# First element of a cached-attention decoder: key tiles scored and reloaded in halves, two more tiles scored earlier, 64 equal columns in the down sums

## The chip, the core and the metric

The kernel runs on one core of one Trainium2 chip, in one launch. The metric is the device time of an execution in microseconds; the times given are medians over runs. Five engines work side by side in a core: TensorE (PE in the profile, its weight loads PEld), VectorE (DVE), ScalarE (ACT), GpSimd (POOL) and SyncE (SP), which in this kernel issues nearly all transfers from HBM. The PE runs at a granted clock that the profile shows in two values, 1.0 and 0.5.

## The reference

Four batch elements, one token each, pass twice through an attention layer (A) and a gated feed-forward layer (B), with the same weights and the same caches both times:

```python
x = A_x                                                    # [4, 1, 512]
x = x + A(layernorm(x));  x = x + B(layernorm(x))
x = x + A(layernorm(x));  x = x + B(layernorm(x))

def A(x):   # 32 query heads on 8 key/value heads, 4096 cached keys, head size 128
    q = (x @ wq).reshape(B, 1, 32, 128).transpose(0, 2, 1, 3)
    k, v = repeat(k_cache, 4, axis=1), repeat(v_cache, 4, axis=1)
    p = softmax(q @ k.T * 128 ** -0.5)
    return (p @ v).reshape(B, 1, 4096) @ wo

def B(x):   # 512 -> 1792 -> 512
    return (gelu(x @ w_gate) * (x @ w_up)) @ w_down
```

All of it is bfloat16. The key cache and the value cache hold 4 x 8 x 4096 x 128 numbers each, 33.5 MB apiece.

## The kernel before, in words

**Units.** A key or value head of one element is two tiles (t = 0 and 1, `last` is 1) of 128 partitions x 16 chunks (`CH`) x 128, 512 KB each: a row of 4096 bytes in each partition. Eight heads make two groups of four (`GH`); for one element and one layer the groups are handled one after the other, called `gx` and `gy`. All tiles of an element's second pass over attention that still lie in SBUF from the first pass are used again, in reversed group order; the rest is loaded again.

**Scores.** `scores_of` (L586) multiplies a key tile by the query block `qb`: four matmuls a tile (`BE`, the loop over `be`), each with 512 moving columns and 32 output rows. Head s writes rows 32s to 32s+31 of the one PSUM tile `sc`, so the matmuls of up to four heads run side by side in the four 32-column strips of the PE; two heads alone use two strips. `qb` is filled by `q_sums_of` (L349, PE) and `q_spread` (L357, DVE) from the rounded query rows `q_bf` of `q_round` (L333, DVE).

**The order of the work** is written out by hand. Each engine runs its instructions in the order of the program, and SP issues the transfers in the order in which they stand. A transfer into a tile waits on SP until the last reader of that place has finished, and all that is behind it on SP waits too. Eight semaphores go round among SP's transfers: one is issued when the transfer eight before it has landed.

**First element, second pass.** `attend_first` (L959) does the first attention of element 0 and then issues all weights (`load_rest`, L158), the down weights `wd_sb` last, and three key tiles of element 1 (`Early`, L1039). `dense_first` (L1314) is the feed-forward layer: gate (L1339), up (L1343), and `down` (L485), 56 matmuls of `wd_sb` with one hidden column repeated to `WIDE` = 32 equal moving columns. `OutProj` (L376) has such repeated columns too, there `WEIGHT` = 64 of them. `busy` (L479) runs matmuls whose result nobody reads. Then `Early.queries` (L1057) makes the query rows of `gx` in two halves of the heads (heads 2 and 3 of the group first), and `Early.scores` (L1089) scores the key tiles of element 0 that were kept in SBUF:

1. `first([(2, 0), (3, 0)])`, and the loads of two key tiles of element 1 into their places;
2. `self.rest()`: query sums and spread for heads 0 and 1;
3. `q = qy()`: the query rows of the other group, `q_rows` (L321): 16 matmuls of 512 columns in all four strips, a DVE transpose of 512 columns, `q_round`;
4. `first([(2, last), (3, last), (0, 0), (1, 0)])`, two more loads, and copies of parked key tiles back from PSUM and spare SBUF (`Parked.back`, L561) by DVE, GpSimd and ScalarE;
5. `first([(0, last), (1, last)])`, a fifth load, more copies; then softmax.

In `attend` (L1135) follow the scores of `gy` (L1170), each with four further loads (L1171), and the value tiles through a ring of eight places (`VRing.pump`, L692).

Of the kernel before, what the change touches and what calls it, by code (L numbers as in the profile page):

```python
# [15 lines left out]
P = 128  # L16
# [3 lines left out]
QS = P // QD  # L20
WIDE = 32
WEIGHT = 64
# [4 lines left out]
CH = 16  # L27
# [9 lines left out]
def kernel(  # L37
# [13 lines left out]
    nc = tc.nc  # L51
# [7 lines left out]
    KD = D // P  # L59
# [8 lines left out]
    W = 4 * QD  # L68
# [20 lines left out]
    dq = nc.sync  # L89
# [5 lines left out]
    wd_sb = wts.tile([P, KF, D], BF16, name="wd_sb")  # L95
# [22 lines left out]
    qb = const.tile([P, W + NK * 2 * W], BF16, name="qb")  # L118
    cs_f = const.tile([P, 2, KF], FP32, name="cs_f")

    place = {(s, t): (KW[s], t) for s in range(GH) for t in range(NT)}
    place.update({(GH + s, t): (KP[t][s // 2], s % 2) for s in range(GH) for t in range(NT)})

    def k_tile(i, t):
        pair, n = place[i, t]
        return pair[:, n]

    def acc(shape, name, t=None):
        if t is None:
            t = ps_ac.tile([P, 512], FP32, name=name, tag="acc")  # L130
        n = 1
        for s in shape:
            n *= s
        if len(shape) == 1:
            return t[:, :n]
        return t[:, :n].rearrange("p (a b) -> p a b", b=shape[1])

    def wide(v, width=WIDE):
        n = v.shape[-1]
        return v.unsqueeze(1).broadcast_to([P, width // n, n])  # L140

    def whole(b, kvh):
        return b == 0 and kvh < GH
# [5 lines left out]
    def cache_tile(cache, b, kvh, t):  # L149
        if whole(b, kvh):  # L150
            return cache[b, kvh].rearrange("(p t c) d -> t p c d", t=NT, p=P)[t]
        return cache[b, kvh].rearrange("(t p c) d -> t p c d", t=NT, p=P)[t]
# [121 lines left out]
    def mac(dst, lhsT, rhs, first, last):  # L274
        nc.tensor.matmul(dst, lhsT=lhsT, rhs=rhs, start=first, stop=last, skip_group_check=True)  # L275
# [37 lines left out]
    def turn_rows(full):  # L313
        flat = full.rearrange("p c r -> p (c r)")
        nc.vector.transpose(out=flat, in_=flat)  # L315
        return full[:, :, :1]
# [13 lines left out]
    def q_tile():  # L330
        return grp.tile([P, HG], BF16, name="q_bf", tag="q_bf", bufs=1)
# [12 lines left out]
    def q_sums(q):  # L344
        qe = q_sum_tile()
        q_sums_of(qe, q, 0, GH)
        return qe
# [9 lines left out]
    def q_spread(qe, s0=0, n=GH):  # L357
        dst = qb[:, W:].rearrange("p (n x a h) -> p n x a h", x=2, a=QD, h=rep)[:, :, 0]
        shape = [P, n * BE, QD, rep]
        nc.vector.tensor_tensor(  # L360
            out=dst[:, s0 * BE:(s0 + n) * BE],
            in0=qe[:, s0:s0 + n].rearrange("p s n h -> p (s n) h").unsqueeze(2).broadcast_to(shape),
            in1=amask.unsqueeze(1).unsqueeze(3).broadcast_to(shape),
            op=ALU.mult)
# [114 lines left out]
    def busy(count, unread, by=None, start=True, lhsT=None):  # L479
        rhs = wg_sb[:, 0] if by is None else by  # L480
        for _ in range(count):
            nc.tensor.matmul(unread, lhsT=ident_bf[:] if lhsT is None else lhsT, rhs=rhs[:, :unread.shape[1]], start=start,  # L482
                             stop=start, skip_group_check=True)

    def down(nb, H_bf, whole):  # L485
        y = acc([KD, WIDE], "y2", whole)
        for c in range(KF):
            for k in range(KD):
                mac(y[:, k], wd_sb[:, c, k * P:(k + 1) * P], wide(H_bf[:, c, :]),
                    c == 0 and k == 0, c == KF - 1)  # L490
        return y[:, :, :nb]


    class Keys:
# [19 lines left out]
        def load(self, count):  # L514
            for _ in range(count):
                kvh, t = self.tile(self.nl)
                self.nl += 1
                dq.dma_start(out=k_tile(kvh, t), in_=cache_tile(A_k_cache, self.b, kvh, t))

        def load_pairs(self, count):  # L520
            for _ in range(count):
                kvh, t = self.tile(self.nl)
                (to, n), (other, m) = place[kvh, t], place[kvh + 1, t]
                if to is not other or (n, m) != (0, 1):
                    self.load(2)
                    continue
                self.nl += 2
                pair = A_k_cache[self.b, kvh:kvh + 2].rearrange("h (t p c) d -> t p h c d",
                                                                t=NT, p=P)
                dq.dma_start(out=to[:], in_=pair[t])  # L530
# [42 lines left out]
    def new_scores(early=False):  # L573
        if early:
            return acc([CH, QS], "sc")
        return ps_sc.tile([P, CH, QS], FP32, name="sc", tag="sc")
# [5 lines left out]
    def scores(sc, g, t, runs=together):  # L582
        for run in runs:
            scores_of(sc, g, [(s, t) for s in run])

    def scores_of(sc, g, run):  # L586
        for be in range(BE):
            for s, t in run:
                n = s * BE + be
                w0 = n * 2 * W + (W if t == 0 else 0)  # L590
                kt = k_tile(g * GH + s, t).rearrange("p c (b j e) -> p c b j e", b=NB, e=2)
                nc.tensor.matmul(sc[s * QS:(s + 1) * QS], lhsT=qb[:, w0:w0 + 2 * W],  # L592
                                 rhs=kt[:, :, be // 2, :, be % 2],
                                 start=(t == 0 and be == 0),
                                 stop=(t == NT - 1 and be == BE - 1))

    def soft(sc, norm=None, lasting=False, meanwhile=None):
# [441 lines left out]
    class Early:  # L1039
# [49 lines left out]
        def scores(self, sc, qy, norm):  # L1089
            gx, gy, own, keys = self.gx, self.gy, self.own, self.keys  # L1090
            a, c, last = gx * GH, gy * GH, NT - 1

            def home(i, t, freed):
                place[i, t] = own[freed]
                return k_tile(i, t).rearrange("p c d -> p (c d)")

            def load(i, t, freed):
                home(i, t, freed)
                assert keys.tile(keys.nl) == (i, t)
                keys.load(1)  # L1100

            def first(run):
                now = {(a + s, t): place[a + s, t] for s, t in run}
                place.update({k: own[k] for k in now})
                scores_of(sc, gx, run)
                place.update(now)

            first([(2, 0), (3, 0)])
            load(a + 3, 0, (a + 2, 0))
            load(a, last, (a + 3, 0))  # L1110
            self.rest()
            q = qy()
            first([(2, last), (3, last), (0, 0), (1, 0)])
            load(a + 1, last, (a + 2, last))
            load(a + 2, last, (a + 3, last))
            to = home(c + 1, last, (a + 1, 0))
            self.one.back(to, 1, nc.vector)
            self.one.back(to, 2, nc.gpsimd)
            self.two[0].back(home(c + 2, last, (a, 0)), 2)
            first([(0, last), (1, last)])  # L1120
            load(a + 3, last, (a, last))
            to = home(c + 3, last, (a + 1, last))
            self.two[1].back(to, 1)
            other = new_scores()

            def build():
                qe = q_sums(q)
                busy(4, other.rearrange("p c j -> p (c j)"))
                q_spread(qe)

            p0 = soft(sc, norm, meanwhile=build)
            self.two[1].back(to, 1, nc.vector)
            return p0, other
# [216 lines left out]
    def dense(b0, y, prev, scr):  # L1350
        nb = 1
        add_x(b0, nb, y)
        prev.fill()
        st = stats(b0, nb)
        add_y(b0, nb, y)
        g = ffn_rows(b0, wg_sb, "g")
        prev.fill()
        rstd, mr = ln_scale(nb, st)
        t = [shifts(scr, mr, i) for i in range(2)]
        sq = gelu(scr, turn_rows(g), t[0], rstd)  # L1360
        u = ffn_rows(b0, wu_sb, "u")
        for _ in range(2):
            prev.fill()
        u = turn_rows(u)
        H_bf = gate_up(scr, sq, u, t[1], rstd)
        prev.whole()
        y = down_rows(H_bf)
        for _ in range(2 if b0 < B - 1 else 1):
            prev.fill()
        return turn_rows(y)  # L1370
# [110 lines left out]
    y, early, scr = attend_first()  # L1481
    prev = NoValues()
    for b in range(B):
        y = dense(b, y, prev, Scratch()) if b else dense_first(y, scr)
        gx, gy = second_groups[b]
# [46 lines left out]
        def qy(b=b, g=gy, norm=norm):  # L1532
            q_bf = q_tile()
            q_round(q_bf, turn_rows(q_rows(b, g)), g, norm)
            return q_bf[:]

        if b < B - 1:
            y, prev = attend(b + 1, qy, prev, norm, early if b == 0 else None)
        else:
            y, full, squares = attend_last(q_bf, norm, prev, late[3 * NT:])  # L1540
# [32 lines left out]
```

## Time and profile before

| what | value |
|---|---|
| median of 3 runs | 267.85 us (267.62 to 268.81) |
| the profiled execution: its own time | 268.99 us |
| the profiled execution: span from first to last instruction | 267.2 us, mean granted clock 0.866 |
| PE, DVE, ACT, POOL busy | 195.1, 182.2, 66.0, 3.9 us |
| read from HBM | 102.50 MB, 384 GB/s over the span |
| q1, the transfers of the kernel | 95.7% of 16 DMA engines' span |
| chain that ended last | DMA 51%, PE 21%, DVE 16% of the span |

Times inside the kernel are us from the span's start; the execution's own time lies 1.8 us above its span. Busy PE time is not PE at its peak, since matmuls overlap; the share of DMA is the mean over 16 engines, and 1.0 means that no engine is without a packet.

### The profile page before, as it was taken

To read this page: it belongs to the slowest core of one execution; us is meant where nothing else is said; L and a number is where in the kernel's file an instruction comes from. 1 tells how busy PE (TensorE), PEld (TensorE's weight loads), DVE (VectorE), ACT (ScalarE), POOL (GpSimd) and SP (SyncE) were. 2 spreads that over 40 slices of the span, in tenths; PEclk is the share of its full clock that TensorE was granted. 3 is DMA by queue.
4 is the path that set the end of the run, shared out by engine and by line. 5 is a ranking of instruction groups with operands and counts; after the bars stand their busy time and mean duration, and the time that the engine had idled before them with its cause. 6 is when DMAs were issued, how large, how long until landed. Compare 5 with 4: busy or idle time off the path is not lost.

```text
span 267.2 us, 8596 instructions
## 1 busy us (share of the span) xinstructions
PE 195.1 (73%) x3767; PEld 114.8 (43%) x3775; DVE 182.2 (68%) x448; ACT 66.0 (25%) x136; POOL 3.9 (1%) x10
## 2 busy tenths in 40 slices
PE   1396246544689796989678968787788687888884
PEld 1333123322255453557436245464363354553563
DVE  3385955451335899884776998746769996568773
ACT  1001001100222422032323520304136103044642
POOL 2000000000001000000000000000000000000001
PEclk9998555655597959799999985899999979999999
DMA  7999999999994999999999999999999999999940
GB/s 244 432 416 421 423 429 417 408 385 406 413 412 177 394 416 417 420 417 400 390 414 416 416 419 421 416 415 375 403 418 418 421 415 418 420 405 405 413 160 3
DMA packets 30732, 103.05 MB, mean 386 GB/s; under 512 B 2788, under 2 KB 7144, under 8 KB 29672
## 3 DMA queue, kind: packets, MB, share of 16 engines
q1 hardware_dynamic: 30672, 102.51, 95.7%
q8 instruction: 29, 0.48, 0.6%
q14 instruction: 7, 0.06, 0.1%
q10 hardware_dynamic: 24, 0.01, 0.0%
HBM read 102.50 MB, written 0.00 MB: 384 GB/s over the span
## 4 chain that ended last, share of the span: by engine, by line
DMA 51%; PE 21%; DVE 16%; SPq 6%; ACT 3%; issue 3%; DVEq 0%
DMA v_t<-in_A_v_cache_dram 25%; DMA kp<-in_A_k_cache_dram 8%; DMA kw<-in_A_k_cache_dram 8%; PE sc L592 6%; DMA wu_sb<-in_B_w_up_dram 5%; DMA kw<-in_A_v_cache_dram 4%; SPq L161 4%; DVE kp L537 3%; PE ot L859 3%; DVE kw L537 3%; PE y L275 3%; PE so L791 2%; PE q L309 1%; DVE q L315 1%; DVE qb L360 1%
## 5 line engine op out<-in xcount | busy, mean ns | idle before, releaser
L592 PE MATMUL sc<-kw,qb 128*32 128x512 bf16 x244 | 39.6, 446 | 5.2 <-DVE kw L537 2.2
L592 PE MATMUL sc<-kp,qb 128*32 128x512 bf16 x268 | 40.1, 450 | 1.0 <-DVE kp L537 0.2
L592 PEld LDWEIGHTS <-qb 128*32 128x32 bf16 x512 | 23.1, 104 | 39.6 <-issue 21.4
L537 DVE STREAM_TRANSPOSE kw<-kw 128x1024 f32<-128x1024 f32 x32 | 38.0, 1215 | 0.7 <-DMA kw<-in_A_k_cache_dram 0.6
L537 DVE STREAM_TRANSPOSE kp<-kp 128x1024 f32<-128x1024 f32 x32 | 36.7, 1199 | 0.0
L859 PE MATMUL ot<-pe,v_t 128*128 128x32 bf16 (+1 forms) x896 | 30.0, 184 | 5.6 <-DMA v_t<-in_A_v_cache_dram 2.8
L859 PEld LDWEIGHTS <-v_t 128*128 128x128 bf16 x896 | 27.7, 100 | 13.7 <-issue 7.4
L614 ACT ACTIVATE pe<-sc,nl 128x512 bf16<-128x512 f32 x8 | 5.5, 687 | 85.9 <-DVE pe L611 67.6
L791 PE MATMUL so<-v_t,pe 128*32 128x256 bf16 x304 | 15.0, 319 | 13.6 <-DMA v_t<-in_A_v_cache_dram 11.6
L799 DVE STREAM_TRANSPOSE so<-so 128x512 f32<-128x512 f32 (+1 forms) x23 | 13.8, 599 | 11.1 <-PE so L791 11.1
L791 PEld LDWEIGHTS <-pe 128*32 128x32 bf16 x320 | 9.1, 105 | 19.4 <-issue 12.5
L602 DVE TENSOR_REDUCE pe<-sc 128x1 f32<-128x512 f32 x12 | 8.3, 691 | 9.2 <-PE sc L592 9.1
L405 PE MATMUL yr<-wo_sb,OT_bf 128*2 128x512 bf16 (+1 forms) x120 | 10.7, 425 | 4.9 <-DMA wo_sb<-in_A_wo_dram 4.9
L647 PE MATMUL x<-pe,ident_bf 128*32 128x128 bf16 x192 | 5.4, 233 | 11.8 <-DVE pe L622 11.8
L647 PEld LDWEIGHTS <-ident_bf 128*32 128x32 bf16 x256 | 5.3, 100 | 16.1 <-issue 14.1
L791 PE MATMUL so<-v_t,pl 128*32 128x256 bf16 x192 | 9.4, 275 | 3.3 <-DMA v_t<-in_A_v_cache_dram 3.3
L650 ACT CAST pe<-x 128x512 bf16<-128x512 f32 x12 | 7.0, 586 | 17.4 <-PE x L647 17.4
L275 PE MATMUL q<-xb,wq_sb 128*128 128x5 bf16 (+1 forms) x192 | 5.7, 173 | 6.5 <-DMA wq_sb<-in_A_wq_dram 6.5
L353 PE MATMUL qe<-q_bf,ident_bf 128*32 128x16 bf16 (+1 forms) x272 | 5.7, 176 | 5.6 <-DVE q_bf L335 2.9
L622 DVE STREAM_TRANSPOSE pe<-pe 128x512 bf16<-128x512 bf16 x12 | 8.4, 696 | 1.1 <-ACT pe L614 1.1
L275 PEld LDWEIGHTS <-wo_sb 128*128 128x128 bf16 x160 | 7.6, 101 | 3.3 <-DMA wo_sb<-in_A_wo_dram 2.6
L482 PEld LDWEIGHTS <-ident_bf 128*128 128x128 bf16 x63 | 5.2, 99 | 8.7 <-issue 4.3
(172 smaller groups left out, 255.2 us busy)
## 6 DMA issues: line engine op xcount, KB each, us to landing
v_t<-in_A_v_cache_dram SPq DMA_DIRECT2D x89, 512.0 KB, 8.5
kp<-in_A_k_cache_dram SPq DMA_DIRECT2D x32, 512.0 KB, 9.9
kw<-in_A_k_cache_dram SPq DMA_DIRECT2D x24, 512.0 KB, 9.6
wq_sb<-in_A_wq_dram SPq DMA_DIRECT2D x2, 2048.0 KB, 7.7
kw<-in_A_k_cache_dram SPq DMA_DIRECT2D x4, 1024.0 KB, 11.6
v_t<-in_A_v_cache_dram SPq DMA_DIRECT2D x4, 1024.0 KB, 14.2
wo_sb<-in_A_wo_dram SPq DMA_DIRECT2D x4, 1024.0 KB, 12.0
wq_sb<-in_A_v_cache_dram SPq DMA_DIRECT2D x3, 1024.0 KB, 11.8
```

Of the source, the lines that this page charges most:

```text
L161: dq.dma_start(out=wo_sb[:, i * n:(i + 1) * n], in_=wo_dram[:, i * n:(i + 1) * n])
L275: nc.tensor.matmul(dst, lhsT=lhsT, rhs=rhs, start=first, stop=last, skip_group_check=True)
L405: nc.tensor.matmul(self.rows[j:j + x.shape[1]], lhsT=x, rhs=wo_sb[:, i], start=self.n < QD, stop=True, skip_group_check=True)
L537: nc.vector.transpose(out=words, in_=words)
L592: nc.tensor.matmul(sc[s * QS:(s + 1) * QS], lhsT=qb[:, w0:w0 + 2 * W], rhs=kt[:, :, be // 2, :, be % 2], start=(t == 0 and be == 0), stop= ...
L602: nc.vector.tensor_reduce(out=m, in_=sc.rearrange("p c j -> p (c j)"), axis=AX.X, op=ALU.min if norm else ALU.max)
L622: nc.vector.transpose(out=flat, in_=flat)
L647: nc.tensor.matmul(x[a * QS:(a + 1) * QS, s], lhsT=ident_bf[:, s * QS:(s + 1) * QS], rhs=pT[:, a], start=True, stop=True, skip_group_check ...
L650: nc.scalar.copy(out=pe, in_=x.rearrange("p s t c h -> p (s t c h)"))
L791: nc.tensor.matmul(ps[d, :NW * QS], lhsT=x[:, w:w + NW].rearrange("p c h -> p (c h)"), rhs=v[:, i:i + NW, d], start=first and i == 0, stop ...
L799: nc.vector.transpose(out=flat, in_=flat)
L859: nc.tensor.matmul(self.ot[:, s % 2], lhsT=v[:, i, :], rhs=wide(pe[:, s, t * CH + i, :], self.ot.shape[-1]), start=(done == 0 and i == 0), ...
```

## The change

It touches four places, all of them used in the first element only, but for `scores_of`, whose new argument leaves the other callers as they were.

- `down` of `dense_first`: the hidden column is repeated to 64 equal columns in place of 32.
- `scores_of` takes a range of the 16 chunks; with half of them a matmul has 256 moving columns.
- Step 1 of `Early.scores`: the two tiles are scored by their first eight chunks, then two half loads (256 KB, rows of 2048 bytes) are issued, one into each freed half; then the same with the second eight chunks. The tiles loaded, their places and their order are as before.
- Steps 3 and 4: tiles (2, last) and (3, last) are scored, and the two loads into their places issued, ahead of the query rows of the second group; (0, 0) and (1, 0) stay behind these.

```diff
     def down(nb, H_bf, whole):
-        y = acc([KD, WIDE], "y2", whole)
+        y = acc([KD, WEIGHT], "y2", whole)
...
-                mac(y[:, k], wd_sb[:, c, k * P:(k + 1) * P], wide(H_bf[:, c, :]),
+                mac(y[:, k], wd_sb[:, c, k * P:(k + 1) * P], wide(H_bf[:, c, :], WEIGHT),
...
+        def load_part(self, kvh, t, part):
+            dq.dma_start(out=k_tile(kvh, t)[:, part],
+                         in_=cache_tile(A_k_cache, self.b, kvh, t)[:, part])
...
-    def scores_of(sc, g, run):
+    def scores_of(sc, g, run, part=slice(0, CH)):
...
-                nc.tensor.matmul(sc[s * QS:(s + 1) * QS], lhsT=qb[:, w0:w0 + 2 * W],
-                                 rhs=kt[:, :, be // 2, :, be % 2],
-                                 start=(t == 0 and be == 0),
+                nc.tensor.matmul(sc[s * QS:(s + 1) * QS, part], lhsT=qb[:, w0:w0 + 2 * W],
+                                 rhs=kt[:, part, be // 2, :, be % 2],
+                                 start=(t == 0 and be == 0 and part.start == 0),
...
-            first([(2, 0), (3, 0)])
-            load(a + 3, 0, (a + 2, 0))
-            load(a, last, (a + 3, 0))
+            new = {(a + 3, 0): own[a + 2, 0], (a, last): own[a + 3, 0]}
+            for part in (slice(0, CH // 2), slice(CH // 2, CH)):
+                first([(2, 0), (3, 0)], part)
...
+                for tile in new:
...
+                    keys.load_part(*tile, part)
...
             self.rest()
-            q = qy()
-            first([(2, last), (3, last), (0, 0), (1, 0)])
+            first([(2, last), (3, last)])
             load(a + 1, last, (a + 2, last))
             load(a + 2, last, (a + 3, last))
+            q = qy()
+            first([(0, 0), (1, 0)])
```

More of the change, by code (lines that the diff above doesn't have):

```diff
@@ L1100, in load, with first @@
                 keys.load(1)
-            def first(run):
+            def first(run, part=slice(0, CH)):
                 now = {(a + s, t): place[a + s, t] for s, t in run}
                 place.update({k: own[k] for k in now})
-                scores_of(sc, gx, run)
+                scores_of(sc, gx, run, part)
                 place.update(now)
-            first([(2, 0), (3, 0)])
-            load(a + 3, 0, (a + 2, 0))
-            load(a, last, (a + 3, 0))
+            new = {(a + 3, 0): own[a + 2, 0], (a, last): own[a + 3, 0]}
+            for part in (slice(0, CH // 2), slice(CH // 2, CH)):
+                first([(2, 0), (3, 0)], part)
+                before = {k: place[k] for k in new}
+                place.update(new)
+                for tile in new:
+                    assert keys.tile(keys.nl + list(new).index(tile)) == tile
+                    keys.load_part(*tile, part)
+                place.update(before)
+            place.update(new)
+            keys.nl += len(new)
             self.rest()
-            q = qy()
-            first([(2, last), (3, last), (0, 0), (1, 0)])
+            first([(2, last), (3, last)])
             load(a + 1, last, (a + 2, last))
             load(a + 2, last, (a + 3, last))
+            q = qy()
+            first([(0, 0), (1, 0)])
             to = home(c + 1, last, (a + 1, 0))
```

## The prediction

> **What bounds the kernel now.** I read the page first, its slices of the span and the chain, then the stretch that stands out in windows of one microsecond, then SP's and PE's timelines there, and last the clock by its own windows.
>
> ```profile
> DMA  7999999999994999999999999999999999999940
> GB/s 244 432 416 421 423 429 417 408 385 406 413 412 177 394 416 417 420 417 400 390 414 416 416 419 421 416 415 375 403 418 418 421 415 418 420 405 405 413 160 3
> ```
>
> A slice is 6.68 us. The transfers run at 375 to 432 GB/s in all but the ends and the thirteenth slice, 177 GB/s. With 102.5 MB to read, the kernel is bound by its transfers: an idle microsecond of them is lost, unless they later wait for an engine. The chain agrees where it names late transfers, which queue for long:
>
> ```profile
> 144.23 10.48 DMA kw<-in_A_k_cache_dram
> 154.78 10.09 DMA v_t<-in_A_v_cache_dram
> ...
> 246.32 11.96 DMA kw<-in_A_v_cache_dram
> ```
>
> The hole by itself (the last columns are granted clock, DMA share, GB/s):
>
> ```profile
> 80.00:81.00 1.00, 1.00 (x48) 0.95 (x45) 0.44 (x2) 0.38 (x2) 0.00 (x0) 0.50 0.59 234
> 81.00:82.00 1.00, 1.00 (x18) 0.44 (x16) 0.30 (x2) 0.00 (x0) 0.00 (x0) 0.50 0.16 66
> 82.00:83.00 1.00, 1.00 (x20) 0.42 (x20) 0.00 (x0) 0.00 (x0) 0.00 (x0) 0.50 0.00 0
> 83.00:84.00 1.00, 1.00 (x30) 0.73 (x28) 0.41 (x3) 0.00 (x0) 0.00 (x0) 0.93 0.00 0
> 84.00:85.00 1.00, 1.00 (x22) 0.54 (x14) 0.83 (x2) 0.00 (x0) 0.00 (x0) 1.00 0.84 291
> ```
>
> Nothing is moved from 81.9 to 84.07, where the first packet comes, 0.97 us after SP issues. SP had waited 7.3 us, and PE's scoring of step 1 is what it waited for:
>
> ```profile
> 69.92 4.37 SPq L518 DMA_DIRECT2D kw<-in_A_k_cache_dram  x3
> 83.10 3.20 SPq L518 DMA_DIRECT2D kp<-in_A_k_cache_dram  x5
> 88.10 2.31 SPq L518 DMA_DIRECT2D kw<-in_A_k_cache_dram  x5
> ```
>
> ```profile
> 81.18 0.61 PE L592 MATMUL sc<-kp,qb 128*32 128x512 bf16 x2
> ...
> 82.44 0.63 PE L592 MATMUL sc<-kp,qb 128*32 128x512 bf16 x2
> ```
>
> The last pair of step 1 starts at 82.44 and takes 0.63: 83.07, and the load goes out at 83.10. The pairs follow each other at 0.427 us, at half clock; at full clock 512 columns take 0.216 (the query rows from 83.21 on).
>
> ```profile
> 76.31:79.73 3.42, 2.96 (x87) 2.41 (x86) 0.93 (x6) 0.00 (x0) 0.00 (x0) 1.00 1.05 420
> 79.73:83.14 3.41, 3.41 (x89) 2.19 (x89) 0.89 (x4) 0.41 (x2) 0.00 (x0) 0.50 0.30 121
> 83.14:86.55 3.41, 3.36 (x61) 1.95 (x52) 2.69 (x8) 1.45 (x2) 1.16 (x2) 1.00 0.66 249
> ```
>
> The clock changes on a grid of 3.41 us. It is full in the window of `down`, half in just the window in which the hole lies.
>
> **The 64 columns.** At full clock the 32-column matmuls of `down` start every 25 ns, while 32 columns stream for 13.5 (0.216 x 32/512). The 64-column ones of the output sums at 124.3 start every 29 to 32 ns. So 56 of them would cost 56 x 5.5 = 0.31 us uncovered. They are covered: the last 16 wait for the pieces of `wd_sb`, which land just ahead of 77.81, 78.15 and 78.45. The first 40, from 76.64, end at 77.86 in place of 77.65; only the last four are exposed: 0.04 us. What they add is streaming. Adding up columns at 0.216 us per 512, matmuls side by side counted once, PE streams 36% of the window at 76.31; 56 x 13.5 = 0.76 us more makes 58%. In this trace full-clock windows with up to 26% were all followed by half clock, those from 39% up never, those between either way (36% and 38% fell, 32 to 34% and another 38% stayed). I take full clock from 79.73 to 83.14.
>
> **The halves.** Scoring starts at 81.2, after `q_spread`. A round of 256 columns takes 0.109 us and its matmul 0.273 (the value sums of L791 at 118): four rounds of the first half start at 81.19 to 81.52 and end at 81.79. The first load goes out at 81.82 in place of 83.10: **1.28 us earlier**. With the clock still half it would be 81.2 + 3 x 0.213 + 0.42 = 82.26, 0.83 earlier. The second half ends at 82.2. SP needs some 0.43 us from issue to issue (83.10 to 83.52), a half takes 256 KB / 412 GB/s = 0.64 us, so four issues to 83.1 keep up.
>
> The price: packets of 2048 bytes (the down weights) take 84 ns, of 4096 bytes 159. 512 small for 256 large ones on 16 engines: (512 x 84 - 256 x 159) / 16 = 0.14 us. Two more transfers take two of the eight semaphores; six tiles' worth in flight is still 7.6 us of work. [...]
>
> **The two tiles ahead of the query rows.** (2, last) and (3, last) alone use two strips for four rounds: 4 x 0.216 = 0.86 us on PE that before ran beside (0, 0) and (1, 0). Step 1 at full clock gives back the like: PE is done with it and with the 16 sums of `rest` at 82.27, the pair of tiles streams to 83.1 and ends at 83.31, and their loads go out at 83.53 and 83.95 in place of 85.02 and 85.44. The query rows end at 84.16 (before 84.08). Behind them the same DVE chain: transpose 0.73, rounding 0.23, copy back 0.69, reduction 0.69, spread 0.42. So the scores of `gy` come 0.07 us later, and the load after them, on which SP waits with everything behind it, at 88.15. The five tiles' data, from 82.8 on at the 380 GB/s that ran from 86 to 90, last to 89.9; the new ones come at 88.15 + 0.97 = 89.1. By 0.8 us, no second hole; but the queue is thin and engines run out unevenly (before, 80.5 to 81.9). Between 0 and 0.3 us, I take 0.1.
>
> **Where the gain goes.** From 84 to 125 the chain is compute that no transfer waits for. The bytes issued and not landed are 1.5 MB or more at 118 and 130 us; the head start takes 1.28 x 0.41 = 0.5 MB of that. Transfers never stop; an unevenly filled queue may cost 0 to 0.4 us, I take 0.2. After 144 the compute waits for transfers again (the lines above), and carries the gain to the end.
>
> **Sum.** -1.28 + 0.04 + 0.14 + 0.1 + 0.2 = **-0.8 us**, from -1.1 to -0.4 by the bounds. On the profiled execution's own 268.99 us (span 267.2 and 1.8 around it) that is 268.2. The median of the runs stands 1.14 us below that execution; taking the same 0.8 off gives **267.05**, rounded 267.1.
>
> **Rivals.**
>
> *The median run has the full clock already.* The grid is not tied to the kernel's start as far as one trace can tell. Moving it over the trace, PE's streaming falls below 39% only for window ends near 79 to 80 and 81, under half of all positions. The runs, 267.6, 267.9 and 268.8, look like two kinds 1 us apart, as 4 x 0.211 = 0.85 of scoring at half clock would make. Then step 1 ended at 81.18 + 0.65 + 0.39 = 82.22 before; the halves gain 0.4, and packets and thin queues take 0.14 to 0.5 back: -0.1 us, 267.75. Against it: one trace only shows the half clock. [...]
>
> *A second hole: slower.* The early pair of tiles delays the query rows, and with them the loads after `gy`. If the clock stays half from 79.7 to beyond 84, PE's extra four rounds cost 1.71 us, the load of 88.10 goes out at 89.8 and moves data at 90.8, while five tiles from 83.2 end at 90.1: a hole of 0.7 us, and 1.7 us less cushion in the queue at 118 and 130, up to 0.7 more, against 0.83 gained and 0.14 for packets: +0.7 us, 268.55. It decides once the load after `gy` is later than 88.9. For it: PE is the busy engine there. Against it: the window at 83.14 is full even before, with PE streaming 89% of the one before.
>
> *More than the sum.* From 84 to 90 the transfers ran at 361 GB/s, not 412; 0.75 us is lost to a ragged restart of two tiles, a pause and three. If halves and earlier loads fill that, -1.6 us: 266.25. Against it: copies by four engines go on there, and packets themselves are longer.
>
> *Halves pay a fixed cost.* If each of two more transfers paid the 0.97 us from issue to first packet without overlap, 1.9 us: 269.0. Against it: before, loads issued 0.43 to 0.48 apart land without a gap. [...]
>
> **Numbers.** Forecast 0.46, the full clock already 0.25, second hole 0.14, more than the sum 0.12, fixed cost 0.03. The range 266.1 to 268.6 takes in the first four up to their prices. 0.5% is 1.34 us, about what a measurement of this kernel can tell from no change. Faster by that needs nearly the whole gain: most of "more", and a little of the forecast: 0.19. Slower by that, the fixed cost and the bad end of the second hole: 0.11. The rest, 0.70, is within.
>
> **What would show it.** Right: SP's first load of step 1 near 81.8 and four issues 0.43 apart; granted clock 1.0 through 80 to 83; `down` still ending near 78.6; the thirteenth slice near 255 GB/s; the load after `gy` near 88.1 and no zero window before it. Wrong: half clock there still, the first load after 82.3, or windows below 200 GB/s at 88 to 91 or 118 to 131.

## The result, and the profile after

The changed kernel took 269.59 us (median of 13 runs, 268.77 to 270.67), the kernel before, run beside it, 268.12 us (13 runs, 267.43 to 269.61). The ratio is 1.0049, with a 95% interval of 1.0029 to 1.0068: slower by some 1.3 us, where 0.8 us of gain was forecast.

The two profiled executions do not show that difference: 268.81 us own time after (span 267.0), 268.99 before (267.2). The first lies 0.8 us below the median of its kernel, the second 0.9 above the median of its own. So the traces are read for the mechanism, and the repeated runs for the size.

The slices of the page after:

```profile
DMA  7999999999995999999999999999999999999940
GB/s 239 433 415 422 421 430 417 408 386 404 414 414 207 378 411 419 419 417 416 385 411 418 417 415 421 417 417 376 377 417 416 420 418 417 420 410 411 421 163 3
```

The thirteenth slice moved up from 177 to 207 GB/s, not to the forecast's 255, and the fourteenth went down from 394 to 378. SP's timeline there:

```profile
82.06 1.75 SPq L521 DMA_DIRECT2D kp<-in_A_k_cache_dram  x4
83.90 1.88 SPq L518 DMA_DIRECT2D kp<-in_A_k_cache_dram  x3
88.18 1.77 SPq L518 DMA_DIRECT2D kw<-in_A_k_cache_dram  x4
```

The first half load went out at 82.06, 1.04 us before the whole load of the kernel before; the load after `gy` at 88.18 (before 88.10). In windows of one microsecond (the last columns are granted clock, DMA share, GB/s):

```profile
82.00:83.00 1.00, 1.00 (x38) 0.72 (x32) 0.26 (x2) 0.00 (x0) 0.00 (x0) 1.00 0.00 0
83.00:84.00 1.00, 1.00 (x24) 0.63 (x22) 0.15 (x3) 0.00 (x0) 0.00 (x0) 1.00 0.85 301
84.00:85.00 1.00, 1.00 (x16) 0.43 (x8) 0.53 (x1) 0.44 (x1) 0.38 (x1) 1.00 0.81 299
85.00:86.00 1.00, 0.71 (x20) 0.27 (x17) 0.96 (x4) 1.00 (x2) 0.79 (x2) 1.00 0.79 236
86.00:87.00 1.00, 0.82 (x3) 0.29 (x3) 1.00 (x4) 1.00 (x2) 0.00 (x0) 1.00 0.95 330
87.00:88.00 1.00, 1.00 (x20) 0.45 (x19) 0.93 (x6) 0.73 (x2) 0.00 (x0) 1.00 0.96 348
```

The clock is full, the first packet comes at 83.03 instead of 84.07, and then the data crawl: 299 and 236 GB/s at a DMA share of 0.8, although three whole loads had been issued by 85.5. From 83 to 88 it moved 301 + 299 + 236 + 330 + 348 = 1514 KB. Before, the window from 84 had 291 GB/s, and those behind it:

```profile
85.00:86.00 1.00, 1.00 (x25) 0.60 (x22) 0.89 (x3) 0.90 (x1) 0.84 (x2) 1.00 0.87 340
86.00:87.00 1.00, 0.86 (x3) 0.20 (x2) 1.00 (x3) 1.00 (x3) 0.33 (x1) 1.00 0.95 385
87.00:88.00 1.00, 1.00 (x19) 0.42 (x19) 0.93 (x5) 1.00 (x3) 0.00 (x0) 1.00 1.05 393
```

From 84 to 88 that is 291 + 340 + 385 + 393 = 1409 KB. A lead of one microsecond, 0.4 MB, is down to 0.1 MB, 0.25 us.

### The profile page after: what moved, and what is told of

It reads as the page before. It is cut to its first block, busy times and chain, and to the rows that moved or that the text cites. A ratio compares the mean times of both kernels' runs of the same rounds, so it can differ in the third digit from the quotient of the medians.

```text
span 267.0 us, 8618 instructions
## 1 busy us (share of the span) xinstructions
PE 192.1 (72%) x3775; PEld 113.8 (43%) x3783; DVE 182.1 (68%) x448; ACT 66.1 (25%) x136; POOL 3.9 (1%) x10
## 4 chain that ended last, share of the span: by engine, by line
DMA 45%; PE 23%; DVE 20%; SPq 5%; issue 3%; ACT 2%; DVEq 0%
DMA v_t<-in_A_v_cache_dram 28%; DMA kp<-in_A_k_cache_dram 8%; PE sc L596 5%; DVE kp L541 5%; DMA wg_sb<-in_B_w_gate_dram 5%; DVE kw L541 4%; PE ot L863 4%; DMA kw<-in_A_k_cache_dram 4%; SPq L161 4%; PE y L275 3%; PE so L795 2%; DVE q L315 2%; DVE pe L606 1%; DVE qb L360 1%; PE q L309 1%
## 5 line engine op out<-in xcount | busy, mean ns | idle before, releaser
L596 PE MATMUL sc<-kw,qb 128*32 128x512 bf16 x244 | 38.6, 446 | 5.4 <-DVE kw L541 2.8
L596 PE MATMUL sc<-kp,qb 128*32 128x512 bf16 (+1 forms) x276 | 38.1, 405 | 1.5 <-DVE kp L541 0.5
L795 PE MATMUL so<-v_t,pe 128*32 128x256 bf16 x304 | 14.7, 311 | 14.5 <-DMA v_t<-in_A_v_cache_dram 12.0
L353 PE MATMUL qe<-q_bf,ident_bf 128*32 128x16 bf16 (+1 forms) x272 | 5.1, 175 | 5.7 <-DVE q_bf L335 2.8
```

The source lines that it names most:

```text
L596: nc.tensor.matmul(sc[s * QS:(s + 1) * QS, part], lhsT=qb[:, w0:w0 + 2 * W], rhs=kt[:, part, be // 2, :, be % 2], start=(t == 0 and be == ...
L795: nc.tensor.matmul(ps[d, :NW * QS], lhsT=x[:, w:w + NW].rearrange("p c h -> p (c h)"), rhs=v[:, i:i + NW, d], start=first and i == 0, stop ...
```

## The experiments

Each ratio is against the kernel before on the same chip, in five rounds, with its 95% interval. Packet times, and the bytes that had landed by some time, are counted over the packets of each trace. A trace is one execution; the ratios come from all.

**One part at a time.** Three theories of the loss: the half loads (H), the 64 columns (C), the order of tiles and query rows (O).

`e1_cols` has the first edit alone:

```diff
-        y = acc([KD, WIDE], "y2", whole)
+        y = acc([KD, WEIGHT], "y2", whole)
```

> Only the 64 equal columns in the down sums; halves and order as before. Theory H (the half loads are what costs): ratio to before 0.997 to 1.000, since only executions that had the half clock in the scoring of step 1 gain their 0.85 us. Theory C (the columns cost: where the clock is still half during the down sums, 56 matmuls start every 53 ns in place of 27 and delay all behind them by about 1.1 us): ratio 1.002 to 1.005. Theory O (the early pair of tiles costs): as theory H.

Measured 1.0001 [0.9982, 1.0021]. `e2_halves` has step 1 alone in halves, scoring and loads:

```diff
-            first([(2, 0), (3, 0)])
-            load(a + 3, 0, (a + 2, 0))
-            load(a, last, (a + 3, 0))
+            for part in (slice(0, CH // 2), slice(CH // 2, CH)):
+                first([(2, 0), (3, 0)], part)
...
+                    keys.load_part(*tile, part)
```

> Only the halves of step 1; 32 columns, and the second pair of tiles behind the query rows as before. Theory H: half loads move slower than whole ones (in the changed kernel 1 MB of halves took from 83.0 to 86.8 us, 276 GB/s), so ratio 1.001 to 1.005, and the profile shows 2048-byte packets with fewer than 16 in flight right behind the restart. Theories C and O: 0.998 to 1.000, the restart 0.4 to 0.8 us earlier.

Measured 1.0044 [1.0021, 1.0068], with the first half load at 81.69. `e3_order` has steps 3 and 4 alone:

```diff
-            q = qy()
-            first([(2, last), (3, last), (0, 0), (1, 0)])
+            first([(2, last), (3, last)])
             load(a + 1, last, (a + 2, last))
             load(a + 2, last, (a + 3, last))
+            q = qy()
+            first([(0, 0), (1, 0)])
```

> Only the order: the pair (2, last), (3, last) and its two loads ahead of the query rows. Theory O: the query rows and all of the second group come 0.86 to 1.7 us later, the load after the second group's scores goes out at 89 or later, ratio 1.002 to 1.006. Theories H and C: ratio 0.999 to 1.002, because the loads behind the second group still find a filled queue.

Measured 0.9996 [0.9966, 1.0026]. `e4_no_cols` is the change with `WIDE` put back in `down`.

> The whole change without the 64 columns. Theory C: the loss goes, ratio 0.997 to 1.001. Theory H and theory O: the loss stays, ratio 1.003 to 1.007, or more, since the scoring of step 1 then runs at half clock in part of the executions.

Measured 1.0042 [1.0015, 1.0069]. The halves alone carry the whole loss; C and O fall. `e3_order` answers a second question. It has 32 columns in `down` and whole loads, and its SP timeline and windows read:

```profile
82.19 3.21 SPq L518 DMA_DIRECT2D kp<-in_A_k_cache_dram  x5
87.81 2.23 SPq L518 DMA_DIRECT2D kw<-in_A_k_cache_dram  x5
```

```profile
83.00:84.00 1.00, 1.00 (x21) 0.49 (x17) 0.00 (x0) 0.00 (x0) 0.00 (x0) 1.00 0.83 225
84.00:85.00 1.00, 1.00 (x12) 0.32 (x6) 0.85 (x2) 0.80 (x1) 0.73 (x2) 1.00 1.01 365
85.00:86.00 1.00, 0.54 (x20) 0.38 (x19) 1.00 (x3) 1.00 (x2) 0.43 (x1) 1.00 1.02 397
86.00:87.00 1.00, 1.00 (x12) 0.34 (x14) 0.96 (x4) 1.00 (x2) 0.00 (x0) 1.00 0.91 336
87.00:88.00 1.00, 1.00 (x23) 0.34 (x19) 0.84 (x4) 0.74 (x3) 0.00 (x0) 1.00 0.96 385
```

The clock is full without the columns, and its first load goes out at 82.19, not 83.10. So the profile shown of before was one with the clock half in that window, which another execution need not have; among the 15 profiled kernels here with 32 columns it came twice more, in `f3_contig` and `g1_quarters` below, and in none of the three with 64. And these whole loads, 0.13 us later than the halves of the change, moved 225 + 365 + 397 + 336 + 385 = 1708 KB by 88, against 1514.

**Scoring or loading, and what of the loading.** The halves split both. `f1_split_scores` scores in halves and loads whole, `f2_split_loads` the other way round:

```diff
-            first([(2, 0), (3, 0)])
+            for part in (slice(0, CH // 2), slice(CH // 2, CH)):
+                first([(2, 0), (3, 0)], part)
             load(a + 3, 0, (a + 2, 0))
             load(a, last, (a + 3, 0))
```

> Step 1 scored in halves, but each of its two tiles loaded whole, after both halves; all else as before. Theory L (the half loads cost, not the half matmuls): ratio to before 0.999 to 1.001. Theory S (the split scoring costs): 1.003 to 1.006, as with the halves alone (1.0044).

```diff
             first([(2, 0), (3, 0)])
-            load(a + 3, 0, (a + 2, 0))
-            load(a, last, (a + 3, 0))
+            for part in (slice(0, CH // 2), slice(CH // 2, CH)):
...
+                    keys.load_part(*tile, part)
```

> Step 1 scored whole as before, then the two tiles loaded by four half loads in the order of the change. Theory L: ratio 1.004 to 1.008, the loss of the halves (1.0044) without the 0.4 us earlier start; a trickle of 2048-byte packets with fewer than 16 in flight behind the restart. Theory S: 0.999 to 1.001.

Measured 1.000 [0.9975, 1.0025] and 1.0038 [1.0011, 1.0066]: it is the loads. Two kernels part what differs in them: L1, that a half takes 2048 bytes out of every 4096 in memory; L2, that there are two more transfers. `f3_contig` loads each half from 256 KB that lie together:

```diff
+            rows = A_k_cache[self.b, kvh].rearrange("(t h p c) d -> t h p c d", t=NT, h=2, p=P)
+            dq.dma_start(out=k_tile(kvh, t)[:, part], in_=rows[t, part.start * 2 // CH])
```

> The halves alone, but each half load reads 256 KB that lie together in HBM (rows of 2048 bytes one behind the other) in place of the first or second 2048 bytes of every 4096; the keys of these two tiles so come in another order than their values. Theory L1 (reading every second 2048 bytes is what is slow): ratio 0.997 to 1.000. Theory L2 (the small rows or the two transfers more are slow by themselves): 1.003 to 1.006, as the halves alone.

`f4_rows2k` keeps two whole transfers, each made of rows of 2048 bytes from two such stretches:

```diff
+                rows = A_k_cache[keys.b, i].rearrange("(t h p c) d -> t p h c d", t=NT, h=2, p=P)
+                dq.dma_start(out=k_tile(i, t).rearrange("p (h c) d -> p h c d", h=2), in_=rows[t])
```

> As before, with the two loads of step 1 whole, one transfer each, but moved in rows of 2048 bytes that lie in two stretches of 256 KB in HBM; the keys of the two tiles so come in another order than their values. If rows of 2048 bytes cost by themselves: 1.003 to 1.006. Theory L1, and a cost of the two transfers more: 1.000 to 1.001, the 0.14 us of the smaller packets.

(In both, the keys of these tiles stand in another order than their values.) Measured 1.0024 [0.9993, 1.0054], which decides nothing between L1 and L2, and 0.9996 [0.9968, 1.0024]: the small rows by themselves cost nothing that can be measured. The trace of `f3_contig` had the clock half in the scoring, and its first half load went out at 82.22, where the prediction reckoned 82.26 for that case.

**More transfers, and another place.** `g1_quarters` is `f2_split_loads` with eight quarter loads (1024 bytes a partition), `g2_quarters_contig` the same from 128 KB that lie together:

```diff
-            for part in (slice(0, CH // 2), slice(CH // 2, CH)):
+            for part in (slice(i, i + CH // 4) for i in range(0, CH, CH // 4)):
```

> Step 1 scored whole; each of its two tiles loaded in four quarters (eight transfers of 128 KB, 1024 bytes of every 4096 in HBM). Twice the suspected dose of the half loads alone (1.0038). Theory L1 (reading with gaps in HBM): 1.006 to 1.012. Theory L2 (each transfer more costs when the queue is refilled from empty): 1.006 to 1.012 too. If neither, 1.003 to 1.005, as with halves.

> As the quarters, but each quarter reads 128 KB that lie together in HBM (the keys of two tiles come in another order than their values). Theory L1: 0.999 to 1.002, the small rows alone. Theory L2: as the quarters before it, 1.006 to 1.012.

Measured 1.0092 [1.0062, 1.0122] and 1.0082 [1.0047, 1.0117]. The loss grows with the number of transfers, 1.0 us for two more and 2.5 for six, 0.4 to 0.5 us each with the smaller packets counted in, and lying together saves nothing that can be measured: L1 falls. `g3_elsewhere` and `g4_elsewhere_contig` load 24 other key tiles in halves, those behind the scores of `gy` in elements 1 to 3, where megabytes are queued:

```diff
-            keys.load(GH)
+            keys.load_halves(GH)
```

> As before, but the 24 key tiles loaded behind the second group's scores of elements 1 to 3 go in halves (2048 bytes of every 4096); the queue is mostly filled there. Theory L2: 0.999 to 1.004, for the smaller packets take 24 x 0.07 = 1.7 us of 16 engines at most. Theory L1: 1.012 or more, if a gap in HBM costs per byte what step 1's halves cost (0.8 us for two tiles, 24 tiles 9 us). If each transfer more costs anywhere: 1.012 or more, here and in the next.

> The same 24 tiles in halves that each lie together in HBM (their keys come in another order than their values). Theory L1: 1.003 to 1.007 (the smaller packets), and well below the run before. Theory L2: as the run before it, 0.999 to 1.007. If each transfer more costs anywhere: 1.012 or more.

Measured 1.0043 [1.0016, 1.007] and 1.0058 [1.003, 1.0087], 1.2 and 1.6 us for 24 more transfers. The smaller packets are enough to explain that: 24 x (256 x 84 - 128 x 159) / 16 ns = 1.7 us. The window from 95 to 120 in `g3_elsewhere`, and then in the kernel before:

```profile
95.00:120.00 25.00, 20.25 (x332) 10.99 (x331) 22.66 (x42) 3.85 (x10) 0.00 (x0) 0.89 1.01 394
```

```profile
95.00:120.00 25.00, 21.34 (x354) 12.08 (x358) 23.28 (x43) 4.42 (x10) 0.00 (x0) 0.83 1.03 417
```

The engines stay busy, at a lower rate. So in these kernels a further transfer costs 0.4 to 0.5 us where the queue is refilled from empty, and no more than its packets where the queue is full.

**What of a transfer costs it.** In `g1_quarters` SP alone cannot keep the queue filled. Its timeline and windows:

```profile
83.15 4.52 SPq L521 DMA_DIRECT2D kp<-in_A_k_cache_dram  x8
87.77 1.33 SPq L518 DMA_DIRECT2D kp<-in_A_k_cache_dram  x3
```

```profile
85.00:86.00 1.00, 1.00 (x27) 0.61 (x22) 0.86 (x3) 0.88 (x1) 0.81 (x2) 1.00 0.79 251
86.00:87.00 1.00, 0.89 (x3) 0.21 (x3) 1.00 (x3) 1.00 (x3) 0.35 (x1) 1.00 0.70 216
87.00:88.00 1.00, 0.96 (x19) 0.44 (x19) 0.93 (x5) 1.00 (x3) 0.00 (x0) 1.00 0.47 151
```

Eight issues take 4.52 us, one of them alone 1.30, for 1.05 MB, 2.5 us of data at 412 GB/s, and the whole loads wait behind them until 87.77. Theory S puts the loss on that pace, theory R on the transfer itself, theory P on small packets in a queue that is filling. `h1_quarters_two` and `h2_halves_two` issue the parts of the second tile from ScalarE:

```diff
-                    keys.load_part(*tile, part)
+                    keys.load_part(*tile, part, (dq, nc.scalar)[list(new).index(tile)])
```

> Whole scoring and eight quarter loads as before (1.0092 with all eight issued by SP), but the quarters of the second tile are issued by ScalarE, which has no work from 80.5 to 84.2 us, so that two queues issue four each, side by side. Theory S (SP's pace: eight issues of 0.57 us are 4.6 us for 2.5 us of data, so the later whole loads are issued too late): the issues take half as long, 2.3 us, the queue is not starved, and the loss falls from 2.5 us to at most 0.8 us: 1.000 to 1.003. Theory R (each transfer costs some 0.4 to 0.5 us on the side of the DMA engines however it is issued): 1.008 to 1.010 again.

> Whole scoring and four half loads (1.0038 with all four issued by SP), the halves of the second tile issued by ScalarE. Theory S: two issues of SP's instead of four, so that the whole loads behind them are issued 0.95 us sooner, and the loss of 1.0 us is gone: 1.000 or a little below. Theory R: 1.003 to 1.005 again.

Measured 1.0043 [1.0009, 1.0077] and 1.0016 [0.9987, 1.0045]. The queues of `h1_quarters_two`, SP's and ScalarE's:

```profile
82.27 1.76 SPq L521 DMA_DIRECT2D kp<-in_A_k_cache_dram  x4
85.10 2.69 SPq L518 DMA_DIRECT2D kp<-in_A_k_cache_dram  x3
```

```profile
82.31 1.81 ACTq L521 DMA_DIRECT2D kp<-in_A_k_cache_dram  x4
```

Eight issues in 1.8 us: the loss of the quarters falls from 2.5 to 1.2 us, so SP's pace looks like about half of it (the intervals overlap a little). The other 1.2 us stay, (1024 x 46 - 256 x 159) / 16 ns = 0.4 us of them the packets of 1024 bytes. They need not be a price of the transfer itself: SP then waited 1.0 and 1.2 us for earlier transfers to land before it could issue the first and the third whole load, which went out at 85.10 and 87.46, in `e1_cols` at 84.16 and 85.06. For the halves, 1.0 us became 0.4, but both intervals hold both values.

`h3_halves_rows` cuts a tile by partitions, so that the packets stay at 4096 bytes:

```diff
-            dq.dma_start(out=k_tile(kvh, t)[:, part],
-                         in_=cache_tile(A_k_cache, self.b, kvh, t)[:, part])
+            dq.dma_start(out=k_tile(kvh, t)[part],
+                         in_=cache_tile(A_k_cache, self.b, kvh, t)[part])
...
-            for part in (slice(0, CH // 2), slice(CH // 2, CH)):
+            for part in (slice(0, P // 2), slice(P // 2, P)):
```

> Whole scoring and four half loads by SP, but a half is 64 of the 128 partitions with all of its 4096 bytes each, instead of 128 partitions with 2048 bytes: the same number of transfers and of issues, and half as many packets in each transfer, as large as those of a whole load. Theories S and R, which count transfers: 1.003 to 1.005 again. Theory P (it is the small packets in a queue that is filling): 0.999 to 1.001.

Measured 1.0087 [1.0057, 1.0116], which neither side expected. Its windows:

```profile
85.00:86.00 1.00, 0.95 (x11) 0.30 (x4) 0.95 (x3) 1.00 (x2) 0.44 (x1) 1.00 1.07 213
86.00:87.00 1.00, 0.91 (x17) 0.44 (x19) 0.93 (x6) 1.00 (x3) 0.00 (x0) 1.00 0.97 225
87.00:88.00 1.00, 1.00 (x21) 0.33 (x13) 0.45 (x2) 0.97 (x4) 0.00 (x0) 1.00 1.09 225
```

All engines are busy, at half the rate: a packet of 4096 bytes takes some 300 ns instead of 159. 1.05 MB at 225 GB/s instead of 412 is 2.1 us more, and 2.3 were lost. This is another price altogether, so the run says nothing on theory P. For rows of 2048 bytes `f4_rows2k` speaks against P: it brought such packets into the same emptied queue in two transfers, landed 1.05 MB in 3.4 us from the first packet, and lost nothing that can be measured (0.9996, against 1.0038 for `f2_split_loads`, though the intervals touch). For 1024 bytes P stays untested.

`h4_no_halves` is the change without its halves, the version that might have beaten both kernels.

> The change without its halves: down with 64 equal columns and the two tiles scored ahead of the second group's query rows, whole scoring, whole loads. As both parts alone gave 1.000, every theory expects 0.998 to 1.001; it is the version that could beat both kernels, by the 0.4 us of a start that comes earlier only where the clock would have been half: then 0.998.

Measured 1.0007 [0.9985, 1.0029]: no gain, and no loss.

What the transfers had landed by 92 us, in traces in which the clock was full:

| step 1 loads | order as before | two tiles ahead |
|---|---|---|
| whole | 35.43 (`e1_cols`), 35.46 (`f1_split_scores`), 35.58 MB (`f4_rows2k`) | 35.62 (`e3_order`), 35.58 MB (`h4_no_halves`) |
| halves by SP | 35.20 (`f2_split_loads`), 35.50 MB (`e2_halves`) | 35.38 (the change), 35.35 MB (`e4_no_cols`) |
| halves by two queues | 35.48 MB (`h2_halves_two`) | |
| quarters | 34.69 (`g2_quarters_contig`), by two queues 35.22 MB | |

The order helps by some 0.15 MB. Halves issued by SP lose some 0.2 MB, 0.5 us; only `e2_halves`, which starts them 0.6 us sooner, is level with whole loads. 0.5 us is under half of the 1.3 us of the repeated runs. Where the rest goes was not found: later restarts of the queue differ by 0.1 to 0.3 MB between executions of any kernel here, which hides it.

## Why the prediction was wrong

The forecast of 267.05 lies 2.5 us below the measured 269.59: 0.8 us of gain that did not come, a loss of 1.3 to 1.5, and 0.3 because the kernel before itself stood at 268.12 over 13 runs, not 267.85.

**The step that failed is "The halves".** It said that SP needs 0.43 us an issue, a half takes 0.64 us, "so four issues to 83.1 keep up", and put the price at 0.14 us for smaller packets. What the runs show in its place is a loss of 1.0 us for the half loads alone (1.0038 with whole scoring), where whole loads behind scoring in halves lose nothing (1.000). The four issues came 0.42 to 0.48 apart and do keep up by that arithmetic: in `f2_split_loads` the first whole load behind the halves goes out at 84.16, as in `e1_cols` behind whole ones. SP in `f2_split_loads`, its windows, and SP in `e1_cols`:

```profile
82.27 1.75 SPq L521 DMA_DIRECT2D kp<-in_A_k_cache_dram  x4
84.16 2.31 SPq L518 DMA_DIRECT2D kp<-in_A_k_cache_dram  x3
```

```profile
85.00:86.00 1.00, 0.95 (x15) 0.31 (x4) 0.93 (x2) 1.00 (x2) 0.46 (x1) 1.00 0.86 209
86.00:87.00 1.00, 0.90 (x17) 0.45 (x19) 0.93 (x6) 1.00 (x3) 0.00 (x0) 1.00 0.85 274
```

```profile
82.28 3.16 SPq L518 DMA_DIRECT2D kp<-in_A_k_cache_dram  x5
```

The data do not come at 412 GB/s. Between 85 and 87 the 2048-byte packets of `f2_split_loads` took 111 to 124 ns in the mean instead of 84 (the median stays 84: 39 of 224 took over 150), and 13 to 14.5 of 16 engines had one. Until 1.05 MB had landed it took 3.1 to 3.2 us from the first packet with whole loads (`e1_cols`, `e3_order`), 3.7 to 4.1 with halves (the change, `e2_halves`, `e4_no_cols`, `f2_split_loads`, `h2_halves_two`; 3.5 in `f3_contig`), 4.9 with the quarters of `g1_quarters`. The step took a steady rate from a full queue for one that starts empty.

The pace of 0.43 us an issue did not hold behind the halves either. In `f2_split_loads` the issue of the second whole load took 1.40 us, and the third went out at 86.08, in `e1_cols` at 85.06. Such an issue, of 1.06 to 1.40 us, stands in the traces of `e2_halves`, `f2_split_loads`, `f3_contig`, the two kernels whose quarters SP issues, and `h3_halves_rows`; with whole loads in step 1 none from 81 to 90 took over 0.61. The traces of the change and of `e4_no_cols` have none, and these kernels lose as much, so it is not all of the loss; whether it makes the queue slow or comes of it, no run shows.

**The rival that came, at another size.** "Halves pay a fixed cost", at a chance of 0.03 and 1.9 us, had the mechanism's outline: a price for each further transfer, not hidden. It was 0.4 to 0.5 us each, not 0.97. The evidence quoted against it, loads issued 0.43 to 0.48 apart that land without a gap, came from whole loads of 512 KB, where each issue brings 1.3 us of data; a half brings 0.64.

**The term of -1.28 us was mis-sized.** It was reckoned from a start at 83.10, and that belongs to an execution with the clock half. With 32 columns and whole loads, `e3_order` and `f1_split_scores` began at 82.19 and 82.30 with the clock full. Against these, the halves start only 0.1 to 0.6 us sooner (82.06 in the change, 81.69 in `e2_halves`). Where the clock was half, the start did come 0.9 us sooner (82.22 in `f3_contig`, against 83.10). The clock's grid of 3.41 us does not start with the kernel: it has an edge at 79.73 in the trace of before and at 74.78 in that of after, 4.95 us apart, no whole number of its steps. The premise of the first rival, "the median run has the full clock already", fits 12 of the 15 traces with 32 columns, though the kernel before itself has one trace only; 0.25 was then too little for it. Its packets and thin queue, 0.14 to 0.5, were too cheap as well.

**What held, and what only looks so.** The 64 columns cost nothing that can be measured (1.0001). But the pieces of `wd_sb` did not hide them. The groups of PE after:

```profile
77.15 1.89 PE L275 MATMUL y<-words,wd_sb 128*128 128x64 bf16 x56 [0.81 <-DVE words L472]
78.88 0.35 PE L482 MATMUL st<-wg_sb,ident_bf 128*128 128x448 bf16 x1
81.39 0.76 PE L596 MATMUL sc<-kp,qb 128*32 128x256 bf16 x10
```

`down` began 0.5 us later there than before, at 77.15, waited for no piece, and ended at 79.04, not near 78.6. With 32 columns and a start at 77.20, in `f1_split_scores`, the 56 matmuls took 1.61 us: the columns cost PE 0.28 us, near the 0.31 reckoned for the uncovered case and not the 0.04 of the sum. The scoring in halves starts at 81.39, 0.2 us later than forecast. The clock was full from 80 to 83 as forecast, though one cannot credit the columns with it.

The load after `gy` went out at 88.18, forecast 88.15, and there was no second hole; with 0.9996 the order costs nothing that can be measured. That the two times agree is in part luck. In eight traces with the clock full the order moves that load from 87.03 to 87.27 (`e1_cols`, `e2_halves`, `f1_split_scores`, `f2_split_loads`) to 87.81 to 88.18 (`e3_order`, `h4_no_halves`, `e4_no_cols`, the change), and the forecast's 0.07 us was counted from an execution whose scoring ran at half clock.

Packets as such were priced rightly: 0.07 us a tile, as the 24 tiles allow. The 0 to 0.4 us of a ragged queue at 118 to 131 was not measured by itself; it moved 410 GB/s there after, 405 before. None of the signs named for "wrong" came in the trace, though the forecast failed: it named none for a slow refill between 83 and 88.

**Open.** Why a half transfer runs below the rate of a queue that holds enough behind it: SP's pace seems to have about half of it for quarters and is undecided for halves; packets of 2048 bytes alone do not explain it, by `f4_rows2k`; what is left may be the transfer itself, SP's long issues, or its waits for earlier transfers to land.

## What to carry to other kernels

Where a queue has run empty, as here from 82 us, try few and large loads first behind the hole: in these runs, cutting them to start sooner gave 0.1 to 0.6 us of start where the clock was full, and each further transfer cost 0.4 to 0.5 us. Price a transfer from a row with the queue in the same state, and when one trace shows the clock half at the place that a change is to cure, look whether other executions of the same code show it too.

## What the runs showed that was not expected

A transfer into 64 of the 128 partitions ran at 213 to 225 GB/s with all 16 engines busy, where transfers into all 128 ran at 412 in the slice ahead of the hole (the page before), and at 393 and 401 behind it (`e1_cols`, 84 to 86). What halves the rate, no run shows.

Where the queue is full, cutting 24 loads in two cost no more than its smaller packets take, 1.2 to 1.6 us for 24; where it is empty, two cuts cost 1.0 us.
